# Chunk-selected attention with a gated causal convolution: the convolution cut into tiles of 64 by 32, output stores moved to ScalarE's queue, values loaded and cast by GpSimd's transfers

## The chip, the cores and the metric

The kernel runs on one core of a Trainium2 chip. The metric is the device time of one launch in microseconds (us). Before the change three runs took 195.68, 196.44 and 196.68 us, so the median is 196.44 us. The profile below is of a separate execution, whose span from the first to the last instruction is 196.0 us, with the TensorE clock fully granted throughout.

## What is computed

There are 4 sequences of 768 positions, 8 heads of 64 channels each. Every block of 32 keys is a chunk. Each query takes its six best chunks, by an upper bound of the score, and attends only to those (and only backwards in time). The heads laid side by side give `x` (4, 768, 512), and this goes through a gated unit: a causal convolution over five positions, channel by channel, gives the gate; `x @ w_val` gives the value; their product goes through `w_out`.

```python
k_min, k_max = min and max of k over each chunk of 32
ub = sum(maximum(q * k_min, q * k_max), axis=-1)         # bound of each chunk, per query
top_chunks = argsort(where(causal, ub, -1e9))[..., -6:]  # six chunks
scores = q @ k.T / sqrt(64), masked to those chunks and to the past
x = softmax(scores) @ v                                  # heads side by side: (4, 768, 512)

gate_pre = sum over k in 0..4 of conv_w[k] * xp[:, k:k + S, :]   # xp: x with four zeros ahead
gate = 1 / (1 + exp(-gate_pre))
out = (gate * (x @ w_val)) @ w_out
```

## The kernel before

Two heads are one pair; there are 16 pairs, four to a sequence. Each pair passes through the same stages. An operation is put on a list with its engine and its buffers, a list scheduler in the program orders all of them ahead of time, and each engine then runs its own fixed order. The keys of that order (`OFF`, `DELTA`, `PERIOD`) are tuned numbers. What runs when is fixed in the program; waits are only for data and buffers.

The loads and the cast of v:

```python
for x, name in enumerate(("kn", "qn", "vn")):
    G.op(f"{name}{p}", "SP", ..., load(name), w=[(name, p)], ...)       # SyncE's queue (L519, L522)

def vcast(p=p):                                                          # L639
    t.nc.gpsimd.tensor_copy(out=vv("VA", p)[:, :, :, 0:D], in_=vv("vn", p))
```

The selection mask is written twice, for two strips of rows (L716):

```python
for r in range(2):
    t.nc.vector.tensor_tensor(out=NS...[:, :, :, CH * r:CH * r + NCH], in0=src, in1=<sixth best>, op=ALU.is_lt)
```

Scores. The 2688 columns of a pair lie in six PSUM banks for each of its two heads (`BANKS`), and two banks make a `DUO`. Per duo, first all products of q and k in tiles of 64 rows (L748), two heads side by side in the array; then the mask is added as a product of 32 rows (L757), four tiles of 32 rows side by side:

```python
DUO = ((0, 1), (2, 3), (4, 5))
WIDTH = [512, 512, 512, 512, 384, 256]
...
for r, bi in enumerate(bs):
    ...
        for hh in range(2):
            t.nc.tensor.matmul(out=bank(("s", p, bi, hh))[:, col:col + n], lhsT=kh[HP[hh], ...], rhs=qh[HP[hh], q0:q0 + n], ...)
...
            for hh in range(2):
                rows = slice(64 * hh + 32 * r, 64 * hh + 32 * r + 32)
                t.nc.tensor.matmul(out=..., lhsT=t.E[rows, ...], rhs=mt[rows, ...], tile_position=(64 * hh + 32 * r, 0))
```

Then ScalarE takes the exponential (L766), GpSimd cuts the diagonal blocks (L774), TensorE multiplies by v (L797), VectorE normalizes (L806), and a transposing transfer puts the result into `xT` (L827).

The convolution is done on TensorE with diagonal weights, in one of two ways:

```python
CONV = "QQQQQQQQQQQSSSSQ"       # which of the ways each pair takes

# Q (L883): tiles of 64 rows by 64 columns, four side by side; needs the two halves of xT swapped (L849)
for k in range(2 * KSZ):
    for x, d in ((xT, 0), (XQ, 1)):
        for r in range(2):
            matmul(out=bank(("cv", p, r))[HP[r ^ d], 0:HB], lhsT=WQ[HP[r], ...], rhs=x[HP[r], a:a + HB])   # 40 of 384 columns

# S (L863): tiles of 128 rows by 32 columns, four side by side; needs four shifted copies, through DRAM
xw: scr[p % 4].rearrange("c (g n) -> g c n", g=4) <- xT        # L839, one transfer
xs: XS[blk::4] <- scr[p % 4]                                   # L845, four transfers
for w in range(2):
    for o in range(3):
        for g in range(4):
            matmul(out=bank(("cv", p, w))[32 * g:32 * g + 32, 0:HB], lhsT=WD[:, ...], rhs=XS[:, ...])       # 24 of 384 columns
```

Value and output, once for each sequence of four pairs: 8 groups of four matmuls with `w_val` (L913), the gate on VectorE (L921), 6 groups of four matmuls with `w_out` (L937), ScalarE takes them out of PSUM (L947; three of the 24 are VectorE's, L944), and SyncE's queue stores them:

```python
t.nc.sync.dma_start(out=t.out[b_, s * 128:(s + 1) * 128, :], in_=vv("osb", 6 * b_ + s))   # L952
```

In the first 26 us gaps of TensorE are filled with matmuls of zeros (L352, L1011).

Of the kernel before, what the change touches and what calls it, by code (L numbers as in the profile page):

```python
# [11 lines left out]
FP = mybir.dt.float32  # L12
# [7 lines left out]
CH = 32  # L20
# [4 lines left out]
KSZ = 5  # L25
NPAIR = B * H // 2
# [7 lines left out]
XN = S + 6  # L34

# [15 lines left out]

DUO = ((0, 1), (2, 3), (4, 5))
SCORE = [0.68, 0.70, 0.54]
# [3 lines left out]
for _bi, _segs in enumerate(BANKS):  # L57
    for _col, _jt, _q0, _n in _segs:
        for _i in range(_n // 128):
            WHERE[_jt, _q0 // 128 + _i] = (_bi, _col + 128 * _i)  # L60

NBUF = dict(kn=5, qn=5, vn=5, Kh=3, Qh=3, ql=2, rh=2, rl=2, km=2, KB=2, VA=3, mub=2, top=2, NS=2,
            MT=2, on=2, xT=8, XS=3, XQ=3, g=8, gv=8, osb=4, scr=4)

PERIOD = 12.9223
OFF = dict(wdg=199.168, wbig=-116.538, cw=-683.48, load=-91.162, ktr=-51.291, qtr=99.521, kev=-172.346,
           qev=175.061, ksm=-204.505, spl=464.719, vc=678.633, ub=-186.285, top=322.7, selT=-163.727,
           sc=-181.883, ex=-292.07, av=82.464, nrm=333.712, tox=-546.25, xs=-141.243, conv=13.848,
           tanh=-338.872, val=266.063, gv=171.155, out=288.504, ev=-184.148)
# [11 lines left out]
CONV = "QQQQQQQQQQQSSSSQ"  # L81

DELTA = dict(
    wdg=(-1.243, -0.346, -5.29, 3.059, -8.51, 0.295, -11.031, 1.615, 2.466, -0.239, -5.796, 0, -2.239, 11.59,
        -0.038, 0),
    wbig=(0, 0.188, -10.953, -0.19, 0.733, -1.414, -3.353, 1.285, -5.523, -4.485, 38.175, 5.823, 4.557,
        -13.478, 0.421, 0),
    cw=(-18.314, -8.891, -8.843, -0.026, -0.2, 7.762, 12.344, 5.613, 0.06, -2.242, -4.873, -3.047, -3.366,
        0.828, -9.749, -0.011),
    load=(0.214, -1.353, 0.394, -9.477, -20.991, -15.326, -0.566, -8.721, 0.066, -10.887, 23.08, 13.879, 6.207,  # L90
        -4.098, -7.797, -2.716),
    ktr=(3.721, -2.57, -4.059, 0.646, -13.55, 0, 0.055, -1.62, -0.373, 0.436, -1.532, 6.05, 2.065, 1.379, 2.36,
        0.267),
    qtr=(-5.316, -3.862, 0.606, 2.517, 0.494, 0.207, -0.25, -17.411, 1.198, 7.239, -4.482, 0.617, -1.715,
        -0.705, 1.938, 2.43),
    kev=(0, -2.085, -0.198, 0.772, 0.854, 1.732, -0.381, -2.561, 0.048, 6.873, -0.748, -3.931, -1.54, -5.598,
        0, 0),
    qev=(-0.006, -7.153, 2.8, -8.078, -1.913, -4.426, -6.52, -0.93, -1.584, 0.557, 6.224, 0.433, 0, 0.167,
        0.325, 1.843),
    ksm=(-0.516, 1.719, 1.719, 0, -8.166, 5.024, -7.553, -5.823, 0, -13.821, -3.788, 0, 0, 0, 6.169, -3.771),  # L100
    spl=(0, 0, 0.913, -1.823, 3.174, 0.698, 2.737, 0, -0.344, -1.736, -3.55, 8.03, 12.699, 0.056, 12.489, 1.296),
    vc=(-5.408, 8.102, -1.641, -3.236, -11.492, -2.331, -9.437, 2.42, -16.561, 6.032, 0, -2.029, 9.507, 2.124,
        11.374, 1.314),
    ub=(0, 5.87, -1.717, -6.846, -10.954, -7.75, -4.319, 18.215, 2.367, -3.332, -1.487, -3.834, 2.838, -3.08,
        -3.376, 6.316),
    top=(0.011, -14.157, -0.748, -6.694, 0, 1.128, -0.085, 25.804, -19.326, 6.323, 7.216, 7.115, 6.031, 0,
        17.873, -1.714),
    selT=(0.159, 4.322, -11.032, -3.664, 2.206, 2.91, 4.105, -0.067, 0, 2.718, -8.959, -6.512, 0.16, 8.002,
        -0.12, -1.732),
    sc=(2.402, 2.062, 3.966, 0.001, -31.282, -1.168, -3.404, 9.113, -1.06, 0.639, 4.728, -3.231, -1.122,  # L110
        -0.658, -0.515, 0.885),
    ex=(-2.337, 0.461, 5.963, 6.189, 0.222, 2.13, 5.144, 9.503, 6.939, 0.624, 0.959, -13.542, -6.471, -4.563,
        6.731, -4.322),
# [206 lines left out]
def graph(off, period, nbuf):  # L320
# [649 lines left out]
    for o in later:  # L970
        o.deps.add(byname["ksm1"])
# [170 lines left out]
```

## Time and profile before

| what | value |
|---|---|
| median of three runs | 196.44 us |
| span of the profiled execution | 196.0 us |
| TensorE (PE) busy | 184.8 us, 94% |
| VectorE (DVE) busy | 148.3 us, 76% |
| ScalarE (ACT) busy | 146.7 us, 75% |
| GpSimd (POOL) busy | 90.4 us, 46% |
| transfers | 36.01 MB, 94917 packets, of which 88226 are under 512 B |
| share of the 16 DMA engines' span taken by SyncE's queue | 74.5% |

A busy time says how long an engine had something in work, not that each piece was as fast as it could be; several matmuls overlap. What bounds the kernel is read from stretches of time: where one engine has no gap at all, its work sets the pace. The chain of work that ended last, and the waits of each engine, show the rest.

### The profile page before, as it was taken

The page shows a single profiled execution, that of the slowest core. Times are in us where ns is not written, and L with a number is a line of the kernel's source. Part 1 is how long each engine was busy: PE and PEld are TensorE (multiplying, and loading weights), DVE is VectorE, ACT ScalarE, POOL GpSimd, SP SyncE. Part 2 cuts the span into 40 slices and gives each one's busy share as a digit, 9 for nine tenths or more (in the row PEclk, how much of TensorE's full clock was granted, in tenths as well). Part 3 has the DMA queues.
Part 4 walks back from the last instruction along what each step waited for, and adds up shares of the span by engine and source line. Part 5 has one row for each costly group of instructions (what it writes and reads, how often), then busy time and mean ns, then how long its engine had stood idle before and what let it go on. Part 6 is the DMA issues. An engine that isn't in the chain of part 4 may idle for free.

```text
span 196.0 us, 7461 instructions
## 1 busy us (share of the span) xinstructions
PE 184.8 (94%) x2926; PEld 118.4 (60%) x2926; DVE 148.3 (76%) x476; ACT 146.7 (75%) x326; POOL 90.4 (46%) x189
## 2 busy tenths in 40 slices
PE   7989898979999999999999999999999997899992
PEld 3666666656757675686675677577656462555540
DVE  6897588979999988879998558998899614062451
ACT  4458999989778879895969897677988977633421
POOL 5589999888445344547262137414363212100000
PEclk9999999999999999999999999999999999999999
DMA  5999999989989998969796998230218839777225
GB/s 134 269 269 207 163 211 205 255 161 225 236 147 222 151 279 190 262 142 222 198 257 181 251 221 162 58 70 2 47 48 251 117 92 282 221 261 251 106 110 211
DMA packets 94917, 36.01 MB, mean 184 GB/s; under 512 B 88226, under 2 KB 91298, under 8 KB 94882
## 3 DMA queue, kind: packets, MB, share of 16 engines
q1 hardware_dynamic: 93826, 34.48, 74.5%
q0 software_dynamic: 1056, 1.05, 3.8%
q8 instruction: 23, 0.38, 0.8%
q14 instruction: 12, 0.10, 0.2%
HBM read 24.16 MB, written 7.08 MB: 159 GB/s over the span
## 4 chain that ended last, share of the span: by engine, by line
PE 74%; DVE 12%; DMA 5%; ACT 4%; SPq 2%; issue 2%; DVEq 0%
PE b L883 10%; PE b L913 10%; PE b L937 9%; PE b L797 9%; PE b L748 8%; PE b L534 8%; PE b L757 5%; PE b L652 5%; DMA xT<-on 3%; DVE km L546 3%; ACT P L766 2%; DMA XS<-scr 2%; PE b L726 2%; PE b L1011 2%; PE b L352 2%; DVE NS L716 2%
## 5 line engine op out<-in xcount | busy, mean ns | idle before, releaser
L766 ACT ACTIVATE P<-b 128x512 f16<-128x512 f32 (+1 forms) x192 | 88.9, 570 | 9.8 <-PE b L757 4.7
L774 POOL TENSOR_SCALAR_AFFINE_SELECT P<-P 128x512 f16<-128x512 f16 (+1 forms) x64 | 33.8, 550 | 60.5 <-ACT P L766 60.4
L546 DVE TENSOR_REDUCE km<-b 128x12 f32<-128x384 f32 x64 | 31.9, 548 | 6.7 <-PE b L534 2.8
L748 PE MATMUL b<-Qh,Kh 64*128 64x128 f16 (+3 forms) x384 | 28.8, 258 | 0.9 <-ACT P L766 0.4
L797 PE MATMUL b<-VA,P 128*128 128x65 f16 x672 | 28.0, 194 | 0.5 <-ACT P L766 0.4
L797 PEld LDWEIGHTS <-P 128*128 128x128 f16 x672 | 24.8, 98 | 4.1 <-issue 1.8
L921 DVE SCALAR_TENSOR_TENSOR gv<-g,b 128x384 f16<-128x384 f32 x32 | 17.5, 550 | 10.2 <-PE b L913 9.1
L913 PE MATMUL b<-xT,wval 128*128 128x384 f16 x128 | 23.8, 326 | 0.0
L937 PE MATMUL b<-wout,gv 128*128 128x512 f16 x96 | 23.5, 379 | 0.0
L947 ACT ACTIVATE osb<-b 128x512 f32<-128x512 f32 x21 | 12.8, 623 | 13.8 <-PE b L937 11.7
L889 ACT ACTIVATE g<-b 128x384 f32<-128x384 f32 x32 | 14.4, 495 | 10.2 <-PE b L883 7.6
L883 PE MATMUL b<-xT,WQ 64*64 64x384 f16 x240 | 21.8, 325 | 0.0
L883 PE MATMUL b<-XQ,WQ 64*64 64x384 f16 x240 | 21.8, 325 | 0.0
L540 ACT ACTIVATE Kh<-b 128x384 f16<-128x384 f32 x32 | 16.2, 520 | 7.0 <-PE b L534 5.2
L748 PEld LDWEIGHTS <-Kh 64*128 64x128 f16 x384 | 12.0, 94 | 12.8 <-issue 11.3
L806 DVE TENSOR_TENSOR on<-b,rcp 128x384 f16<-128x384 f32 x32 | 17.8, 557 | 1.1
L576 ACT ACTIVATE Qh<-b 128x384 f16<-128x384 f32 x32 | 15.7, 531 | 2.7 <-PE b L534 2.7
L757 PE MATMUL b<-MT,E 32*128 32x128 f16 (+4 forms) x352 | 17.6, 259 | 0.0
L883 PEld LDWEIGHTS <-WQ 64*64 64x64 f16 x480 | 12.8, 106 | 6.8 <-issue 2.0
L913 PEld LDWEIGHTS <-wval 128*128 128x128 f16 x128 | 11.5, 98 | 7.9 <-issue 1.3
L622 DVE SCALAR_TENSOR_TENSOR rl<-Qh,ql 128x640 f16<-128x640 f16 x16 | 15.9, 994 | 0.2
L534 PE MATMUL b<-ident,kn 128*128 128x128 f32 x96 | 15.1, 282 | 0.1
(102 smaller groups left out, 320.8 us busy)
## 6 DMA issues: line engine op xcount, KB each, us to landing
kn<-in_k_dram SPq DMA_DIRECT2D x32, 192.0 KB, 3.7
qn<-in_q_dram SPq DMA_DIRECT2D x32, 192.0 KB, 3.7
vn<-in_v_dram SPq DMA_DIRECT2D x16, 384.0 KB, 5.1
out_dram<-osb SPq DMA_DIRECT2D x24, 256.0 KB, 3.1
XS<-scr SPq DMA_DIRECT2D x16, 193.3 KB, 3.3
XQ<-xT SPq DMA_DIRECT2D x24, 96.8 KB, 2.5
scr<-xT SPq DMA_DIRECT2D x4, 193.5 KB
wval<-in_moe_w_val_dram POOLq DMA_DIRECT2D x1, 512.0 KB, 8.6
```

What stands on the lines that cost most here:

```text
L534: t.nc.tensor.matmul(out=b[:, j * 128:(j + 1) * 128], lhsT=vv(name, p)[:, 3 * w + j, :], rhs=t.ident, is_transpose=True, start=(j == 0), s ...
L546: t.nc.vector.tensor_reduce(out=vv("km", p)[:, i, w * 12:(w + 1) * 12], in_=bank(("kn", p, w))[:, 0:HB].rearrange("p (c t) -> p c t", t=CH ...
L748: t.nc.tensor.matmul(out=bank(("s", p, bi, hh))[:, col:col + n], lhsT=kh[HP[hh], jt * 128:(jt + 1) * 128], rhs=qh[HP[hh], q0:q0 + n], star ...
L757: t.nc.tensor.matmul(out=bank(("s", p, bi, hh))[:, col + m0 - q0:col + n], lhsT=t.E[rows, jt * 128:(jt + 1) * 128], rhs=mt[rows, m0 - 128: ...
L766: t.nc.scalar.activation(out=t.P[p % 2][hh][bi], in_=bank(("s", p, bi, hh))[:, 0:n], func=AF.Exp, scale=0.125 / QS)
L774: t.nc.gpsimd.affine_select(out=ap, in_=ap, pattern=[[0, n], [1, 128]], compare_op=ALU.is_ge, fill=0.0, base=0, channel_multiplier=-1)
L797: t.nc.tensor.matmul(out=b[:, qt, :], lhsT=t.P[p % 2][hh][bi][:, col:col + 128], rhs=vv("VA", p)[:, hh, jt, :], start=(jt == 0), stop=(jt ...
L806: t.nc.vector.tensor_tensor(out=vv("on", p)[:, :, hh * 64:(hh + 1) * 64], in0=b[:, :, 0:D], in1=rc.unsqueeze(2).to_broadcast([128, NT, D]) ...
L883: t.nc.tensor.matmul(out=bank(("cv", p, r))[HP[c], 0:HB], lhsT=t.WQ[HP[r], k // KSZ, k % KSZ, (p % 4) * 2 + c, :], rhs=x[HP[r], a:a + HB], ...
L913: t.nc.tensor.matmul(out=k[:, 0:HB], lhsT=t.wval[:, ct, et * 128:(et + 1) * 128], rhs=t.xT[:, (4 * b_ + ct) % 8, XL + w * HB:XL + (w + 1) ...
L921: t.nc.vector.scalar_tensor_tensor(out=vv("gv", 4 * b_ + et)[:, sl], in0=vv("g", 4 * b_ + et)[:, sl], scalar=1.0, in1=bank(("val", b_, et, ...
L937: t.nc.tensor.matmul(out=k, lhsT=vv("gv", 4 * b_ + et)[:, s * 128:(s + 1) * 128], rhs=t.wout[:, et, :], start=(et == 0), stop=(et == NCT - 1))
```

## The change

What it does and is for:

- **Convolution.** A new way R takes 15 of the 16 pairs (the last stays Q). It uses tiles of 64 rows by 32 columns, eight side by side. It needs two copies of `x`, in two halves of the sequence, which go through DRAM: one write with the 128 partitions as its outer dimension, instead of one with an outer dimension of 4, and four reads. The aim is less time on TensorE for each convolution.
- **Scores.** The duos go. Each of the six banks of a pair is a unit of its own, and the mask is added in tiles of 64 rows, as the products of q and k are. So the mask is written once on VectorE instead of twice.
- **Values.** The load of v and its cast to 16 bits become one transfer issued by GpSimd, which casts on the way. GpSimd's cast and the buffers of the uncast v go; `VA` has five buffers instead of three, k and q six instead of five.
- **Output stores** are issued by ScalarE, except for three of the last sequence.
- **Setup.** GpSimd builds the R weights in five pieces of 512 elements, and only the last pair's Q weights (two of 640 instead of ten of 512); the big weights and these come later.
- All keys of the schedule are tuned anew.

```diff
-NBUF = dict(kn=5, qn=5, vn=5, Kh=3, ..., VA=3, ...)
+NBUF = dict(kn=6, qn=6, Kh=3, ..., VA=5, ...)
-CONV = "QQQQQQQQQQQSSSSQ"
+CONV = "RRRRRRRRRRRRRRRQ"
 ... (PERIOD, OFF and DELTA: new numbers)
-        for x, name in enumerate(("kn", "qn", "vn")):
+        for x, name in enumerate(("kn", "qn")):
+        def vload(p=p, b_=b_, h0=h0):
+            for hh in range(2):
+                t.nc.gpsimd.dma_start(out=vv("VA", p)[:, hh, :, 0:D], in_=t.v[b_, h0 + hh].rearrange("(t p) d -> p t d", p=128))
-        def vcast(p=p):
-            t.nc.gpsimd.tensor_copy(out=vv("VA", p)[:, :, :, 0:D], in_=vv("vn", p))
 ... (mask)
-            for r in range(2):
-                t.nc.vector.tensor_tensor(out=...[:, :, :, CH * r:CH * r + NCH], ...)
+            t.nc.vector.tensor_tensor(out=...[:, :, :, 0:NCH], ...)
 ... (scores: one unit for each bank instead of each duo)
-                                rows = slice(64 * hh + 32 * r, 64 * hh + 32 * r + 32)
-                                t.nc.tensor.matmul(..., lhsT=t.E[rows, ...], rhs=mt[rows, ...], tile_position=(64 * hh + 32 * r, 0))
+                            nc.tensor.matmul(..., lhsT=t.E[HP[hh], ...], rhs=mt[HP[hh], ...])
 ... (convolution)
-            t.nc.sync.dma_start(out=t.scr[p % 4].rearrange("c (g n) -> g c n", g=4), in_=t.xT[:, p % 8, XL - 4:XL + S + 2])
+            t.nc.sync.dma_start(out=t.scr[p % 4], in_=t.xT[:, p % 8, XL - 4:XL + S])
+        def xs(r, p=p):
+                for blk in range(2):
+                    t.nc.sync.dma_start(out=vv("XS", p)[HP[r]][blk::2].rearrange("c (g n) -> c g n", g=4),
+                                        in_=t.scr[p % 4].rearrange("(g c) n -> c g n", g=4)[:, :, HB * r:HB * r + XH])
+        def conv(p=p):
+            for k in range(KSZ):
+                for g in range(4):
+                    for r in range(2):
+                        t.nc.tensor.matmul(out=bank(("cv", p, r))[32 * g:32 * g + 32, 0:HB],
+                                           lhsT=t.WD[HP[r], k * 16 + (p % 4) * 4 + g, :],
+                                           rhs=x[HP[r], g * XH + k:g * XH + k + HB], ...)
 ... (output)
-                t.nc.sync.dma_start(out=t.out[b_, ...], in_=vv("osb", 6 * b_ + s))
+                e = t.nc.sync if b_ == B - 1 and s % 2 else t.nc.scalar
+                e.dma_start(out=t.out[b_, ...], in_=vv("osb", 6 * b_ + s))
```

## The prediction

> **What bounds the kernel now.** I read the page's busy times first, then the stretches, then TensorE's own waits, then the chain.
>
> ```profile
> PE 184.8 (94%) x2926; PEld 118.4 (60%) x2926; DVE 148.3 (76%) x476; ACT 146.7 (75%) x326; POOL 90.4 (46%) x189
> ...
> DMA  5999999989989998969796998230218839777225
> ```
>
> The first line alone does not prove a TensorE bound: fillers and overlapping matmuls count as busy. The stretches do it. Columns: busy us of PE, its weight loads, DVE, ACT and POOL, then the granted clock, the DMA share and GB/s.
>
> ```profile
> 20.00:30.00 10.00, 9.10 (x180) 6.49 (x180) 7.75 (x37) 9.82 (x25) 9.51 (x17) 1.00 1.07 193
> 30.00:40.00 10.00, 9.13 (x175) 6.33 (x173) 9.31 (x28) 9.70 (x23) 9.37 (x15) 1.00 1.09 215
> ...
> 60.00:80.00 20.00, 20.00 (x358) 13.54 (x356) 18.20 (x61) 16.58 (x38) 9.46 (x22) 1.00 1.01 214
> 80.00:100.00 20.00, 20.00 (x346) 13.82 (x341) 18.45 (x59) 17.53 (x40) 9.33 (x20) 1.00 0.85 204
> ...
> 160.00:170.00 10.00, 7.96 (x129) 4.39 (x129) 2.34 (x6) 6.89 (x16) 1.31 (x3) 1.00 0.85 238
> ```
>
> There are three parts. Up to about 50 us no single engine is full: ACT, POOL and DVE take turns at 93 to 98%, and transfers are saturated. From 60 to 160 us TensorE has no gap, with DVE near 90%. After that TensorE is again the engine of the chain, with one hole, which the waits name (us in total, times, longest):
>
> ```profile
> PE b L863 <- DMA XS<-scr: 2.0, 1, 2.0
> PE b L352 <- DVE warm L346: 1.3, 1, 1.3
> PE b L726 <- DVE NS L716: 0.7, 2, 0.4
> ```
>
> So after 50 us a microsecond taken from TensorE is nearly a microsecond of the kernel, as long as the others keep up. The chain in order of time gives the price of its pieces (start, us, what):
>
> ```profile
> 67.80 0.38 PE b L748 x8
> 68.45 0.42 PE b L797 x10
> ...
> 90.79 0.55 PE b L748 x12
> 91.64 1.83 PE b L937 x8
> 93.47 0.54 PE b L748 x4
> 94.33 0.79 PE b L652 x20
> ...
> 103.67 1.75 PE b L883 x40
> ...
> 171.83 1.10 PE b L863 x24
> ```
>
> One Q convolution is 1.75 us, one S convolution 1.10 to 1.17. From the start of a duo to the next piece gives the scores with their mask: 91.64 - 90.79 = 0.85, 94.33 - 93.47 = 0.86, 68.45 - 67.80 = 0.65, in all 2.36 us a pair.
>
> **What the Trainium skill says.** (1) "TensorEngine Tiling (Array Packing)", Available Configurations, lists 64x32 as eight tiles; its Key Properties say that a change of tiling mode drains the engine. The trace agrees: forty Q matmuls of 384 columns, four side by side, need 10 x 384 / 2.4 = 1600 ns of columns (2.4 GHz is the clock that the next page gives) and take 1.75, so about 0.15 us goes at the ends. (2) "TensorE: Matmul & The Clock Gate", section Wait — 56ns, not 53.3ns?, gives about 25 ns as the least distance between matmul starts. Here sixteen small ones (L667) take 0.39 us in the chain, 24 ns each: it agrees. (3) "DMA: Bandwidth & Descriptors", Issuing engines are not separate DMA queues: another issuer saves only issue time, the 16 engines are shared. No run here has stores on ACT yet.
>
> **The change part by part.**
>
> *Convolution.* Eight tiles: 5 x 384 / 2.4 = 0.80 us, plus 0.15 at the ends, 0.95. But 40 matmuls in 0.80 us are 20 ns apart, below the 24 ns just seen: 40 x 24 = 0.96, plus 0.15, 1.11. I take the middle, 1.05 (estimate). Eleven Q become R: 11 x (1.75 - 1.05) = 7.7. Four S become R: 4 x (1.15 - 1.05) = 0.4. **8.1 us off TensorE**, all of it after 50 us.
>
> *Scores.* Now: 2688 product columns at two heads side by side are 1.12 us; the masks over queries from 192 on are 2432 columns a head, in four tiles about 0.56 us (the longer bank of each duo: 448, 512 and 384). Sum 1.68 against 2.36 measured: 0.68 over three duos is lost, which I put down to drains when the tiles go from 64 to 32 rows and back. After: 2688 + 2432 = 5120 columns are 2.13 us, without a change inside a bank. The built program has 49 runs of score matmuls on TensorE against 45 before, so some three entries a pair at about 0.11 each: 2.13 + 0.34 = 2.47. **16 x 0.11 = 1.8 us on.** The choice to drop the duos then costs little, because half of what they saved went in drains.
>
> *DVE.* The mask is written once: half of 24 x 457 + 8 x 399 ns, **7 us off DVE**. From 60 us this is hidden, but it keeps DVE below TensorE at the faster pace: (148.3 - 7) / 16 is 8.8 us a pair, and TensorE's own, without 9.5 us of fillers (3.6 + 5.9) and the 6.3 us net found here, is (184.8 - 15.8) / 16 = 10.6. Before 50 us it counts.
>
> *Start.* k and q of the second pair no longer stand behind a v (0.63 us of issue, 384 KB) in SyncE's queue. GpSimd, 95% full from 20 to 40 us, loses ten Q weight pieces (10.9 us) and the casts (0.83 each), and gains five of about 1.1 and issues. DVE is on the path from 30 to 50 us and saves 0.4 a pair there. **About 2 us off** (estimate, my softest term).
>
> *Values.* The cast goes: 16 x 0.83 = 13.2 us off POOL. 32 issues of 768 rows come; the two weight loads took POOL 0.94 and 0.75 us each, so some 29 us on. POOL ends near 100 of 190 us: free enough. Same packets read, half the bytes written.
>
> *Detour.* Per pair R moves 198 KB out and 4 x 99 KB back, Q swapped 194 KB: 11 x 0.4 - 4 x 0.37 (S moved 967 KB) = +2.9 MB, less 3.1 MB of v written. Near neutral in bytes.
>
> *Stores.* SyncE needs 0.42 to 0.5 us for one. If ACT's queue stands still as long, 21 x 0.45 = 9.5 us, about half of it after 160 us, where ACT is idle. ACT is at 82 to 88% before, so most hides; I add 1.
>
> Sum: -8.1 + 1.8 - 2 + 1 = -7.3, and I take 0.3 back for waits that the new fixed order meets: 196.4 - 7.0 = **189.4 us**.
>
> **Rivals.**
>
> *A: the detour becomes the wait.* Fifteen convolutions now need transpose, write, read in a row, and the DMA share is already about 1.0 from 60 to 80 us. Every landing adds: 2.9 (transpose), about 3 (write: the page has no landing for it, I take it like the read) and 3.3 us (read), and the one wait of TensorE on a transfer now is of this kind (2.0 us). For it: the order is fixed, and a late read stops TensorE at once. Against it: SyncE is relieved of v and stores, the write spreads over 128 outer rows instead of 4, and transfers fall to 11% busy around 135 us, so there is room in total. If it happens a few times: 193 to 197.
>
> *B: ACT becomes the bound.* At a 4% faster pace 85% becomes 89, with 0.45 us a store and its wait for the copy out of PSUM some 94%. Exponentials free the PSUM banks that TensorE needs. Time 191 to 194.
>
> *C: matmuls of 64x32 overlap fully and the start gains more.* R at 0.95 gives 9.6 off instead of 8.1; a start 4 us shorter gives 184 to 186.
>
> *D: casting transfers are slow.* If a packet that casts takes twice the 25 ns mean of now (74.5% of 16 x 196 us over 93826 packets), 24576 of them add 38 us to each engine's 156, and loads come late: above 196. No trace here has small casting packets.
>
> **Range and chances.** The TensorE terms are firm to about 2.5 us; the start is between 0 and 4 off, A and B together between 0 and 5 on. That gives 183.5 to 194.5. Faster by over 2% means below 192.5: 0.78. Within 2%: 0.15. Slower takes A or D in full: 0.07.
>
> **What would show it.** R convolutions at 1.0 to 1.1 us each in the chain; scores near 2.5 us a pair; TensorE without gaps from about 50 us on, fewer us busy in all (near 176: 6.3 of work and some fillers less); DVE near 141; ACT's waits ahead of exponentials short. Wrong it would be by TensorE waits on XS above 4 us in total, by R above 1.3 us, by waits for VA, or by ACT full while TensorE has gaps.

## The result and the profile after

The changed kernel takes **202.24 us** (median of 4 runs, 201.75 to 202.76) where the kernel before took 196.56 beside it: a ratio of 1.030, with an interval of 1.025 to 1.035. It is 5.7 us slower; 189.4 was predicted, and the range ended at 194.5.

First the same two lines of the profile's page that the prediction showed of before, busy times and the slices of the DMA engines, then the page's queues (packets, MB, and their packets' time as a share of 16 engines' span), all of the changed kernel:

```profile
PE 181.0 (90%) x2982; PEld 120.1 (60%) x2982; DVE 138.6 (69%) x456; ACT 144.7 (72%) x326; POOL 97.6 (49%) x200
...
DMA  6999999999999999999979999998941675544325
...
q1 hardware_dynamic: 73714, 25.47, 70.3%
q0 software_dynamic: 26144, 4.20, 30.6%
q10 hardware_dynamic: 3024, 5.51, 7.6%
```

The DMA engines were near full until about 120 us and rested around 135; now they are near full until 145. q1 is SyncE's, q0 GpSimd's and q10 ScalarE's. Together the queues' packets took 109% of the engines' span (79% before, nearly all SyncE's), although the bytes hardly changed: 35.65 MB after 36.01. Over 100% means that packets of different queues were under way at once on one engine.

TensorE's stretches of the changed kernel (columns as in the prediction):

```profile
60.00:80.00 20.00, 19.33 (x393) 14.24 (x390) 18.79 (x72) 17.70 (x42) 16.39 (x33) 1.00 1.58 185
80.00:100.00 20.00, 19.20 (x409) 14.04 (x407) 15.60 (x53) 16.08 (x38) 9.66 (x19) 1.00 1.48 191
100.00:120.00 20.00, 15.30 (x247) 9.44 (x246) 10.28 (x33) 11.80 (x26) 7.80 (x18) 0.94 1.04 207
120.00:140.00 20.00, 20.00 (x317) 13.06 (x316) 14.66 (x42) 14.04 (x32) 5.71 (x12) 0.98 1.17 214
```

Where TensorE had no gap it now has 4.7 us of them between 100 and 120 us, the two longest 2.4 and 1.7 us; DVE, ACT and POOL fall too: everybody waits. Below, the two together are called the hole. The chain of the changed kernel, in order of time, names what ended the longer one, and one convolution later on (start, us, what):

```profile
110.34 0.57 SPq L510
110.92 0.05 issue
110.97 4.91 DMA kn<-in_k_dram
115.87 0.02 issue
115.89 0.02 ACTq L936
...
116.34 0.50 ACT g L872
116.83 0.04 issue
116.88 0.47 PE b L779 x10
...
131.87 0.94 PE b L846 x40
```

A load of k goes out late, at 111 us, and lands at 115.9. What waits for it is no transpose but ACTq L936, a store in ScalarE's stream. Behind the store stand the gate's tanh (L872), and behind that TensorE, 2.44 us. Why a store waits for a load of k is told by the waits of the built program, two transfers of SyncE's and the store:

```
L510 DMACopy kn0_133<-in_k_dram 128x6x64       [waits DMAHW2_49]
L510 DMACopy kn0_133<-in_k_dram 128x6x64       [waits DMAHW3_49]
L936 DMACopy out_0_dram<-osb2_200 128x512      [waits DMAHW3_49,Activation_49]
```

In the built program the 182 transfers of SyncE and ScalarE report their landing on eight counters, DMAHW0 to 7, in turn. Before a transfer may use a counter, its issuer waits until the transfer that used it last has landed, whatever that was; the store is the eighth transfer after the second of these loads. So at most eight of these transfers can be under way, and how fast they land sets how fast the next go out. Stores on ScalarE bring that wait into the engine that makes exponentials.

The timeline of SyncE's queue shows why k went out late (start, us, what; a group of transfers with its own waits):

```profile
93.72 1.17 SPq L510 DMA_DIRECT2D kn<-in_k_dram  x2
94.93 2.37 SPq L510 DMA_DIRECT2D qn<-in_q_dram  x2
97.34 2.06 SPq L510 DMA_DIRECT2D kn<-in_k_dram  x2
99.50 7.31 SPq L826 DMA_DIRECT2D XS<-scr  x8
106.85 0.59 SPq L821 DMA_DIRECT2D scr<-xT  x1
107.55 2.74 SPq L809 DMA_TRANSPOSE xT<-on  x2
110.34 1.18 SPq L510 DMA_DIRECT2D kn<-in_k_dram  x2
```

From 93 to 111 us SyncE has no free moment. Eight reads of the detour, a write and two transposes, 10.6 us of queue, stand between two loads of k. And the transfers are slower: k's median from issue to landing went from 3.7 to 4.7 us, q's from 3.7 to 5.8, the transposes' from 2.9 to 4.4. The runs will show that for k and q this second part comes mostly with the loads of v, and not with the detour.

### The profile page after: what moved, and what is told of

It reads as the page before. It is cut to its first block, busy times and chain, and to the rows that moved or that the text cites. A ratio compares the mean times of both kernels' runs of the same rounds, so it can differ in the third digit from the quotient of the medians.

```text
span 200.1 us, 7601 instructions
## 1 busy us (share of the span) xinstructions
PE 181.0 (90%) x2982; PEld 120.1 (60%) x2982; DVE 138.6 (69%) x456; ACT 144.7 (72%) x326; POOL 97.6 (49%) x200
## 2 busy tenths in 40 slices
DMA packets 102917, 35.65 MB, mean 178 GB/s; under 512 B 89058, under 2 KB 99810, under 8 KB 102882
## 3 DMA queue, kind: packets, MB, share of 16 engines
q1 hardware_dynamic: 73714, 25.47, 70.3%
## 4 chain that ended last, share of the span: by engine, by line
PE 53%; DMA 16%; ACT 9%; SPq 9%; DVE 7%; issue 3%; ACTq 0%; DVEq 0%
PE b L920 10%; PE b L896 9%; PE b L736 7%; DMA qn<-in_q_dram 7%; PE b L527 6%; ACT P L750 6%; PE b L779 6%; PE b L741 5%; PE b L846 5%; SPq L510 5%; DMA XS<-scr 4%; SPq L826 3%; DMA scr<-xT 3%; DMA kn<-in_k_dram 2%; PE b L641 2%
## 5 line engine op out<-in xcount | busy, mean ns | idle before, releaser
L750 ACT ACTIVATE P<-b 128x512 f16<-128x512 f32 (+2 forms) x192 | 89.7, 632 | 7.5 <-PE b L741 6.8
L736 PE MATMUL b<-Qh,Kh 64*128 64x128 f16 (+3 forms) x384 | 39.9, 258 | 1.0 <-issue 0.8
L741 PE MATMUL b<-MT,E 64*128 64x128 f16 (+4 forms) x352 | 37.2, 255 | 1.3 <-DVE MT L722 1.3
L779 PE MATMUL b<-VA,P 128*128 128x65 f16 x672 | 27.9, 194 | 3.2 <-ACT g L872 2.4
L518 POOL DMA_DIRECT2D VA<-in_v_dram x32 | 27.2, 855 | 6.7 <-PE b L779 6.4
L779 PEld LDWEIGHTS <-P 128*128 128x128 f16 x672 | 24.9, 98 | 8.8 <-issue 7.1
L736 PEld LDWEIGHTS <-Kh 64*128 64x128 f16 x384 | 18.2, 94 | 12.3 <-issue 8.1
L872 ACT ACTIVATE g<-b 128x384 f32<-128x384 f32 x32 | 14.6, 524 | 14.9 <-PE b L846 7.7
L896 PE MATMUL b<-xT,wval 128*128 128x384 f16 x128 | 25.3, 334 | 0.0
L930 ACT ACTIVATE osb<-b 128x512 f32<-128x512 f32 x21 | 12.7, 618 | 13.7 <-PE b L920 10.6
L741 PEld LDWEIGHTS <-E 64*128 64x128 f16 x352 | 17.6, 94 | 6.2 <-issue 3.6
L846 PE MATMUL b<-XS,WD 64*32 64x384 f16 x600 | 16.0, 324 | 3.7 <-DMA XS<-scr 2.0
L527 PE MATMUL b<-ident,qn 128*128 128x128 f32 x96 | 14.6, 281 | 2.2 <-DMA qn<-in_q_dram 2.2
L527 PE MATMUL b<-ident,kn 128*128 128x128 f32 x96 | 14.1, 279 | 1.2 <-DMA kn<-in_k_dram 1.2
```

The lines of the kernel that those rows point to most:

```text
L518: t.nc.gpsimd.dma_start(out=vv("VA", p)[:, hh, :, 0:D], in_=t.v[b_, h0 + hh].rearrange("(t p) d -> p t d", p=128))
L527: t.nc.tensor.matmul(out=b[:, j * 128:(j + 1) * 128], lhsT=vv(name, p)[:, 3 * w + j, :], rhs=t.ident, is_transpose=True, start=(j == 0), s ...
L736: nc.tensor.matmul(out=bb[hh][:, col:col + n], lhsT=kh[HP[hh], jt * 128:(jt + 1) * 128], rhs=qh[HP[hh], q0:q0 + n], start=(si == 0), stop= ...
L741: nc.tensor.matmul(out=bb[hh][:, col + m0 - q0:col + n], lhsT=t.E[HP[hh], jt * 128:(jt + 1) * 128], rhs=mt[HP[hh], m0 - 128:q0 + n - 128], ...
L750: t.nc.scalar.activation(out=t.P[p % 2][hh][bi], in_=bank(("s", p, bi, hh))[:, 0:n], func=AF.Exp, scale=0.125 / QS)
L779: t.nc.tensor.matmul(out=b[:, qt, :], lhsT=t.P[p % 2][hh][bi][:, col:col + 128], rhs=vv("VA", p)[:, hh, jt, :], start=(jt == 0), stop=(jt ...
```

## The experiments

Two theories at first. **Transfers**: the detour and the loads of v fill the queue and the engines that k and q need. **TensorE**: the new matmuls or their order cost what the prediction had counted as saved. The last is soon out: the chain's convolution of 0.94 us is better than predicted. So the runs ask which transfers, and by what: SyncE's time to issue, or the packets. Each run gives the median of all its executions and a ratio to the kernel before, run on the same chip; the changed kernel is 1.030. Some executions show a lower TensorE clock or a longer time than the rest, and the ratios leave these out; where too few remain, no ratio is given. Differences in us are worked out from the ratios, times 196.6 us. (Expectations that quote earlier runs took differences of medians: 7.9 us for v, 10.8 to 12.3 for the detour, 4 for the stores.)

### Loads of v left out

The changed kernel; from the sixth pair on v isn't loaded, and later pairs multiply old values.

```diff
         def vload(...):
+            if p >= nbuf['VA']:
+                return
```

> The changed kernel with the loads of v left out from the sixth pair on (old values stay in the buffers); every engine's order as in the changed kernel. Theory V (GpSimd's casting transfers crowd the 16 engines and make k and q land late): the hole of TensorE from 100 to 120 us closes, k and q land in about 3.7 us as in the kernel before, 192 us or less. Theory D (the detour's transfers are the excess): 197 to 200. Theory L (k and q stand too late in SyncE's order): 197 or more, since their place is the same.

Measured: 194.33 us, ratio 0.983 (0.979 to 0.986). 9 us come back, and the landings of k and q fall to 4.1 and 4.4 us.

### The detour left out

The changed kernel; from the fourth pair on, scratch writes and reads aren't made, and convolutions use old copies.

```diff
         def xw(p=p):
+            if p >= nbuf['XS']:
+                return
         def xs(r, p=p):
             def emit():
+                if p >= nbuf['XS']:
+                    return
```

> The changed kernel with the detour's writes and reads left out from the fourth pair on (convolutions take old data); all orders kept. Theory D: k and q land in about 3.7 us, the hole closes, 192 us or less. Theory V: 197 to 200. Theory L: also faster, since SyncE has some 35 us less to issue ahead of the loads, but k and q still land slowly: 194 to 197.

Measured: 191.44 us, ratio 0.973 (0.965 to 0.981): 11 us come back, and TensorE has no gap from 100 to 180 us. The two parts together would give 20 us if they were separate costs.

One half of the expectation failed. The loads of k and q land no sooner than in the changed kernel (4.7 and 5.8 us there; the last number is the median from issue to landing):

```profile
kn<-in_k_dram SPq DMA_DIRECT2D x32, 192.0 KB, 5.1
qn<-in_q_dram SPq DMA_DIRECT2D x32, 192.0 KB, 5.7
```

So the hole closes although the landings stay slow; leaving v out had brought them down. What changes here is when the loads are issued, the last of them at 132.5 us and not at 139.3 as in the changed kernel.

### v by SyncE again

The changed kernel, with v loaded by SyncE and cast by GpSimd as before; the order on TensorE, ScalarE and VectorE is kept. Pair 13 multiplies an older v, because its cast comes after its use.

```diff
-        def vload(...): nc.gpsimd.dma_start(out=VA, in_=v)
+        nc.sync.dma_start(out=vn, in_=v)
+        def vcast(...): nc.gpsimd.tensor_copy(out=VA, in_=vn)
```

> The changed kernel with v loaded uncast by SyncE and cast by GpSimd, as before the change; the orders of TensorE, ScalarE and VectorE kept. Theory V: 193 to 196. Theory D: 199 to 203, as the same packets are still moved. Theory L: 203 or more, since SyncE gets 16 more transfers ahead of its loads.

Measured: 208.5 us, ratio 1.057 (1.047 to 1.068), 5 us slower than the changed kernel. Beside this detour, GpSimd's transfers are the lesser evil. It has one waste in it (16 more issues in a full queue), so it says nothing of v alone.

### Loads of k and q earlier

The changed kernel; the loads of pairs 8 to 15 stand up to 20 us earlier in SyncE's order.

```diff
-    return G, t, G.schedule(), full
+    return G, t, earlier(G.schedule()), full      # LEAD = 20.0
```

> The changed kernel with the loads of k and q of pairs 8 to 15 put up to 20 us earlier in SyncE's order, nothing else moved. Theory L: the hole of 100 to 120 us closes, 193 to 196. Theories V and D: the transfers are full anyway, so the detour comes late instead: 200 to 204.

Measured: 211.1 us (206.75 to 213.77), with no ratio; the fastest execution is still 4 us above the slowest of the changed kernel. The theory that the loads only stand too late in the order finds no support: put forward, they hold up the detour instead. TensorE's waits in an execution of 212 us:

```profile
PE b L846 <- DMA XS<-scr: 7.2, 5, 2.5
PE b L641 <- DVE on L788: 4.5, 1, 4.5
```

In the changed kernel's own order the wait for XS was 2.0 us. What one transfer gains another loses.

### A thin detour

The changed kernel; all the detour's transfers are issued and waited for, but from the fifth pair (writes) and the fourth (reads) with 1/16 of the rows, so that convolutions use partly old copies.

```diff
-  ... dma_start(out=t.scr[p % 4], in_=t.xT[:, ...])
+  n = 8 if p >= nbuf['scr'] else 128
+  ... dma_start(out=t.scr[p % 4][0:n], in_=t.xT[0:n, ...])     # reads: 2 rows of 32
```

> The changed kernel with every write and read of the detour still issued and waited for, but from the fifth pair (writes) and the fourth pair (reads) on with a sixteenth of the rows, so that almost no data moves. If what the detour costs is the data on the 16 engines: 191 to 193, as with the detour left out. If it is SyncE's time to issue 75 transfers and the extra links of its chain: 198 to 202, as with the whole change.

Measured: 194.59 us, ratio 0.985 (0.978 to 0.992). Of the 11 us some 9 go with the data; the other 2, with issues and waits, are within the spread of the two runs. Its SyncE timeline for the same stretch:

```profile
97.96 5.27 SPq L828 DMA_DIRECT2D XS<-scr  x8
...
106.43 1.23 SPq L510 DMA_DIRECT2D kn<-in_k_dram  x2
```

The eight reads hold the queue 5.3 us instead of 7.3, and the next k goes out 3.9 us sooner: with fewer packets to move the queue moves faster. Whether transfers also land sooner can't be read from this trace.

### Stores by SyncE again

```diff
-                e = t.nc.sync if b_ == B - 1 and s % 2 else t.nc.scalar
+                e = t.nc.sync
```

> The changed kernel with all output stores issued by SyncE at the places where ScalarE issued them. If the stores held ScalarE up: 199 or less. If SyncE's queue is the narrow place, as the run with v put back into it suggests: 204 or more. If neither: 201 to 203.

Measured: 198.39 us, ratio 1.004 (1.001 to 1.007). So in the changed kernel stores by ScalarE cost about 5 us, more than the 1 predicted. That is about the size of the hole, which came through two such stores: 2.4 us behind the one shown, and 1.7 behind one that stood until an XS had landed.

### The kernel before, with v by GpSimd alone

The kernel before; v by GpSimd's casting transfers where SyncE loaded it, six buffers, no cast.

```diff
-        nc.sync.dma_start(out=vn, in_=v);  nc.gpsimd.tensor_copy(out=VA, in_=vn)
+        nc.gpsimd.dma_start(out=VA[p % 6], in_=v)
```

> The kernel before with one part of the change alone: v loaded and cast by GpSimd's transfers at the places where SyncE loaded it, six buffers for it, no cast; all other orders kept. If casting transfers crowd the engines: 199 or more. If they relieve SyncE's queue, as the run with v put back suggests: 193 to 196. Else within 1 us of 196.6.

Measured: 202.47 us, ratio 1.029 (1.024 to 1.033): by itself this part costs as much as the whole change. TensorE's first wait, and the stretch of 20 to 40 us, of this run:

```profile
PE b L797 <- POOL P L774: 5.3, 5, 2.4
...
20.00:40.00 20.00, 15.21 (x316) 11.43 (x313) 13.20 (x55) 16.78 (x40) 19.23 (x29) 0.99 1.17 164
```

GpSimd issues 32 transfers at 0.85 us each; here its stretch is full, its cuts of the diagonal (L774) come late, and TensorE waits for them. In the same 20 us TensorE was busy 18.23 us before. The landings of k and q, 3.7 us each before, are 4.4 and 4.8 us in this run, with no new detour in it: slower landings come with these loads of v. In the changed kernel, where GpSimd builds fewer weights, no wait of TensorE names GpSimd.

### The kernel before, with half of Q's work left out

The kernel before; the 12 Q convolutions leave out the correcting half of their weights, 20 matmuls instead of 40.

```diff
-            for k in range(2 * KSZ):
+            for k in range(KSZ):
```

> The kernel before with the second, correcting half of the twelve Q convolutions left out (weights of 16 bits only), so that each takes about 0.95 us instead of 1.75; no transfer and no order changed. If a microsecond of TensorE is a microsecond of the kernel as long as transfers don't grow (the first claim of the prediction): 12 x 0.8 = 9.6 us less, 187 to 189. If VectorE, ScalarE or the loads take over as the bound: 191 to 195.

Measured: 194.03 us, ratio 0.984 (0.979 to 0.990). TensorE has about 12 x 0.8 = 9.6 us less to do, and the kernel gains 3. One stretch suggests the next limit, VectorE at 18.68 of 20 us (18.45 before); it is from the slowest execution of this run, 196.15 us:

```profile
80.00:100.00 20.00, 19.81 (x313) 13.58 (x310) 18.68 (x60) 17.13 (x39) 10.11 (x22) 1.00 1.06 234
```

### The same, with the second mask copy left out

```diff
-            for r in range(2):        # mask, L716
+            for r in range(1):
```

> The kernel before with the correcting half of the 12 Q convolutions left out (9.6 us less TensorE work, which alone brought only about 3 us), and with the second copy of the block mask left out on VectorE, as the changed kernel has it (0.3 to 0.45 us per pair, some 6 us of VectorE in all). The second mask rows then keep old contents; the work on TensorE is the same. Theory VectorE (with TensorE relieved, VectorE at 18.7 to 18.9 of 20 us is what holds the kernel before): 188 to 191 us, 3 to 6 us below the run without the mask change. Theory transfers (with TensorE relieved, loads and the swap's landings hold it): 193 to 195 us, within 1 us of that run.

Measured: 191.43 us, ratio 0.975 (0.967 to 0.983). The mask, which the prediction had called hidden after 60 us, seems to bring some 2 us more once TensorE is relieved; the two intervals overlap, so this is likely and not shown. Together the two are worth 5 us.

### The kernel before, with stores by ScalarE

```diff
-                t.nc.sync.dma_start(out=t.out[b_, ...], in_=osb)
+                e = t.nc.sync if b_ == B - 1 and s % 2 else t.nc.scalar
+                e.dma_start(out=t.out[b_, ...], in_=osb)
```

> The kernel before with one part of the change: output stores issued by ScalarE at the places where SyncE issued them, every second of the last batch's by SyncE. Theory ScalarE: ScalarE is busy about 70 to 75 percent, and each store puts a wait for the output copy and 0.34 us of issue into its stream, so 1.5 to 4.5 us slower, 198 to 201 us. Rival (a hidden cost because TensorE has slack against ScalarE in the kernel before): within 1 us, 196 to 197.5 us.

Measured: 198.38 us, ratio 1.006 (1.003 to 1.008): 1.1 us by the ratio. Both theories had missed it a little; the prediction's 1 us holds in the old order.

### The changed kernel without detour

The changed kernel in its own order; each convolution is done as Q with the upper half of the weights alone, 20 matmuls, with the swap where the detour's reads stood. It leaves out the correcting half, so weights count as 16-bit numbers, as x does.

```diff
         def conv(p=p):
+            return convq(p)
 ... convq
-            for k in range(2 * KSZ):
+            for k in range(KSZ):
 ... detour: xw gone; xs(r):
+                t.nc.sync.dma_start(out=vv("XQ", p)[HP[1 - r], :], in_=t.xT[HP[r], p % 8, XL - 4:XL + S + 2])
```

> The changed kernel in its own order, with the detour gone for all pairs: every convolution is done in 64-by-64 tiles as the old Q form, but with the upper 16-bit half of the weights alone, 20 matmuls of 384 columns where Q had 40 and the new form has 40 half-sized ones. So TensorE's work per convolution is about half of Q's 1.75 us, 0.9 us, the same as the new form's 0.94, and the only traffic is the swap of two halves inside SBUF (0.39 MB written per pair in place of 0.19 + 0.39 MB written and as much read). Theory transfers (the detour's packets crowd out the loads of k and q): as in the run that left the detour out from the fourth pair on, 190 to 192.5 us, landings of k and q between the old 3.7 and the new 4.7 to 5.8 us, and TensorE without the hole at 100 to 120 us. Theory GpSimd (casting loads of v are what holds the kernel): within 3 us of the changed kernel, 199 or more. Theory TensorE-mode (the tiles of 64 by 32 themselves slow the stream of matmuls): 188 to 190 us, with 100 to 180 us less than the earlier run by the drains.

Measured: **189.92 us**, ratio 0.962 (0.953 to 0.971). With the two runs that follow it is the fastest of the study. Its stretch of 100 to 120 us, and one convolution in its chain:

```profile
100.00:120.00 20.00, 19.87 (x251) 12.32 (x249) 14.42 (x44) 15.71 (x37) 11.12 (x25) 1.00 1.10 172
...
80.72 0.94 PE b L857 x20
```

A convolution takes 0.94 us here as in the changed kernel, and v, stores, scores and mask are the changed kernel's. So the new order and its savings are good for 7 us, once the detour is gone. Most of that is the shorter convolution and the single mask: the kernel before with both (191.43 us, ratio 0.975) is some 2.6 us behind, and the two intervals overlap. As with the detour left out, k and q land no sooner, 5.0 and 5.7 us after issue.

### The same, with stores by SyncE

```diff
-                e = t.nc.sync if b_ == B - 1 and s % 2 else t.nc.scalar
+                e = t.nc.sync
```

> The same without the detour, and with all the output stores issued by SyncE at the same places instead of ScalarE. Theory ScalarE (a store in ScalarE's stream costs its 0.34 us of issue and its wait, about 20 times, in the path of exponentials and evictions): 3 to 4 us under the run beside it, about 187 to 188.5 us, as the stores alone were worth 4 us in the changed kernel. Rival (the stores only mattered because everything behind them was already late through the detour): within 1 us of the run beside it, 190 to 192 us. Rival (SyncE's issues delay the loads once it has stores again): 0 to 2 us slower.

Measured: 190.33 us, ratio 0.967 (0.961 to 0.972), no gain. The 5 us that stores cost beside the detour are gone. ScalarE's waits name no transfer, with stores (the run before this one) or without: when it comes to a store, the counter is free.

### Without detour and without v

The kernel without detour, with v left out from the sixth pair on as in the first run.

```diff
         def vload(...):
+            if p >= nbuf['VA']:
+                return
```

> The kernel without the detour (convolutions in 64-by-64 tiles with the upper half of the weights, 189.9 us) with the loads of v left out as well from the sixth pair on, so that later pairs multiply by older values. In the changed kernel leaving v out was worth 7.9 us and leaving the detour out 10.8 to 12.3 us; what is to be told apart is whether these are two costs or one. Theory sharing (both act through the same full DMA engines, and one relieved leaves room for the other): v is now worth at most 2 us, 188 to 190 us. Theory GpSimd (the casting loads cost by GpSimd's own issue time and packets, whatever else is in flight): 5 to 8 us more, 182 to 185 us.

Measured: 189.23 us, ratio 0.963 (0.959 to 0.967): nothing is gained. With the detour, v was worth 9 us; without it, none, although k and q now land 4.5 and 4.7 us after issue. So the two aren't separate costs. Whether they meet in the DMA engines isn't shown by this: without the detour TensorE has no gap worth naming from 80 us on, and then a load that lands sooner has nothing to give.

### The kernel before, with a detour's traffic added

The kernel before; where it issues a swap, four reads of the size and pieces of the new detour are added in nine pairs, and four scratch writes. Nobody waits for the data.

```diff
         def swap(p=p):
             ...
+            if p < 11:
+                if p < 4:
+                    nc.sync.dma_start(out=dscr[p % 4], in_=xT)
+                if p >= 2:
+                    (four times) nc.sync.dma_start(out=XS[p % 3] half, in_=dscr[(p - 2) % 4])
```

> The kernel before in its own order, with the detour's traffic added and nothing else: in 9 of its first 11 pairs, where the swap is issued, four more transfers of 97 KB from DRAM scratch to the buffers of the shifted copies, in the pieces that the changed kernel reads, and four writes of the scratch for a start; nobody waits for the data, and TensorE's work is unchanged. About 4.3 MB more, all before the loads of k and q end. Theory transfers (packets of the detour crowd the loads out, whoever uses them): 3 to 7 us slower, 200 to 204 us, landings of k and q above 4.2 us (3.7 before). Theory chain (the detour costs by its two landings in a row ahead of the convolution, not by its bytes): within 1 us, 196 to 198 us.

Measured: 213.56 us, ratio 1.088 (1.083 to 1.093). Far more than expected, and not in the expected way: k and q land in 3.7 and 3.8 us, as before. What changed is when they are issued. v in SyncE's queue, in the kernel before and then in this run (ns of one issue, least/median/most; first and last start):

```profile
L519 SPq DMA_DIRECT2D vn<-in_v_dram x16: 386/628/1373, 3.5 to 116.8; - x16
```

```profile
L519 SPq DMA_DIRECT2D vn<-in_v_dram x16: 380/638/5033, 3.5 to 133.9; - x16
L856 SPq DMA_DIRECT2D XS<-dscr x36: 588/612/1627, 57.7 to 148.3; - x36
```

40 added transfers at 0.61 us are 24 us of SyncE's time. The last v goes out 17.1 us later, and the kernel is 17 us longer. The order has no place made for these transfers; one tuned with them might pay less.

### The same, thin

As before, with 2 rows of 32 in each added read.

```diff
-   ... XS[...][blk::2] <- dscr[...][:, :, ...]
+   ... XS[...][blk:4:2] <- dscr[...][0:2, :, ...]
```

> The run of the kernel before with the extra detour traffic (213.6 us), with the 36 added reads cut from 32 rows to 2 each: the same number of transfers is issued by SyncE at the same places, with 1/16 of the data; the four writes of the scratch stay. In that run k and q landed as fast as in the kernel before (3.7 and 3.8 us), but SyncE issued 40 transfers more at about 0.61 us each, 24 us in all, and the last v was issued at 133.9 us instead of 116.8. Theory issue (the time in SyncE's queue is what costs): still 208 to 214 us. Theory data (the packets cost, through full DMA engines): 197 to 202 us.

Measured: 210.22 us, ratio 1.067 (1.055 to 1.079). 13 of the 17 us stay without the data. TensorE's first wait of this run:

```profile
PE b L891 <- DMA XQ<-xT: 8.2, 5, 2.4
```

In the old order the cost of a detour is mostly SyncE's time, and it comes out as waits for swaps that are issued late. The kernel before had no such wait among its longest.

### The loads of k by ScalarE

The changed kernel; the last ten pairs' k is issued by ScalarE at the same places.

```diff
-                    t.nc.sync.dma_start(out=dst[...], in_=src[hh]...)
+                e = t.nc.scalar if name == "kn" and p >= 6 else t.nc.sync
+                    e.dma_start(out=dst[...], in_=src[hh]...)
```

> The changed kernel with the loads of k of the last ten pairs (20 transfers, 0.62 us of issue each in SyncE's queue) issued by ScalarE at the same places of the order; same packets, same buffers, same computation. Theory issue (SyncE's queue in order, full from 50 to 130 us, is what makes the changed kernel late): 12 us leave SyncE's queue and some 7 to 12 us of issue enter ScalarE, which was 72 percent busy; the last q is issued 5 us or more before 139 us and the kernel takes 194 to 199 us. Theory packets (the full DMA engines set when data lands, whoever issues): the loads land no sooner, ScalarE's added issues cost, 201 to 207 us.

Measured: 213.19 us, ratio 1.084 (1.076 to 1.092). Worse than either theory had it, and by another mechanism. The chain of this run (start, us, what):

```profile
97.80 5.74 DMA XS<-scr
103.56 0.38 ACTq L511
104.03 0.50 ACTq L511
```

A landing of the detour holds up a load of k in ScalarE's stream, for the same reason as the stores: the counter isn't free. ScalarE's exponentials stand behind it. k lands later as well, 5.5 us after its issue in the median instead of 4.7.

### Half of the detour's reads by ScalarE

```diff
-                    t.nc.sync.dma_start(out=vv("XS", p)...
+                    e = t.nc.scalar if blk else t.nc.sync
+                    e.dma_start(out=vv("XS", p)...
```

> The changed kernel with every second read of the detour (30 of 60, 0.60 us of issue each) issued by ScalarE instead of SyncE at the same places; same packets and computation. These reads wait for the landing of the scratch's write, in ScalarE's stream now. Theory issue: 18 us leave SyncE's queue, so k and q are issued earlier, 195 to 200 us, unless ScalarE's waits for the writes stop the exponentials. Theory packets: 201 to 206 us.

Measured: 201.16 us (196.83 to 203.71). The times lie too far apart for a verdict: the median is about that of the changed kernel, and one execution is 5 us below it. A gain from this is neither shown nor excluded.

### The detour in fewer transfers

The changed kernel at full precision; two writes lay the scratch out so that one read of 388 KB fills all the copies. It makes three transfers a pair instead of five, with the same data in the copies.

```diff
-   nc.sync.dma_start(out=scr, in_=xT)                              # 1 write
+   for r in range(2): nc.sync.dma_start(out=scr[r].rearrange("c g n -> g c n"), in_=xT[..., half r])
-   (four times) nc.sync.dma_start(out=XS[HP[r]][blk::2], in_=scr rows of 388)
+   nc.sync.dma_start(out=XS, in_=scr.rearrange("r c g n -> (r c) (g n)"), each row twice)
```

> The changed kernel with its own convolution at full precision, order and issuers, and the detour packed anew: two writes of 99 KB lay the scratch out by half, channel and group, and one read of 397 KB, each scratch row of 3104 B going to two rows of the shifted copies, takes the place of four reads of 97 KB in rows of 776 B. Three transfers a pair in place of five, the same bytes into the copies, fewer and larger packets. Each of SyncE's and ScalarE's transfers waits for one of eight counters, so for the landing of a transfer about eight places earlier; fewer transfers turn these over less often. Theory transfers (issue time, packets and the eight counters, all in the stretch of 40 to 130 us): 192 to 197 us, with q1's share below 65 percent and the hole of 100 to 120 us under 2 us. Theory chain (the detour costs by write and read in a row ahead of the convolution): 200 to 204 us, as now.

Measured: 206.58 us (204.48 to 208.64) where the kernel before took 197.13. A miss: no faster than the changed kernel's 202.24. q1's packets still take 71.1% of the engines' span (70.3 in the changed kernel), since the bytes are the same and only 4680 of q1's 73714 packets went. With the thin detour this suggests that in the changed kernel the data count more than the number of transfers. It doesn't show it, because the large read brings a cost of its own: it stands in SyncE's queue until its write has landed, twice for 5.0 us in all.

## Why the prediction was wrong, step by step

**"After 50 us a microsecond taken from TensorE is nearly a microsecond of the kernel": wrong.** The prediction guarded itself with "as long as the others keep up". They don't: 9.6 us less on TensorE gave 3 us, and 5 with the mask. Lines with 20.00 of 20.00 show that TensorE always had something in work, and not that the others had reserve. VectorE at 18 of 20 stood in the same lines; "near 90%" is too much for the whole of 60 to 160 us, though, since from 100 to 120 us it was 14.2 of 20 and from 140 to 160 us 15.0.

**Convolution: better than predicted.** 0.94 us against 1.05, which is rival C's 0.95. The prediction had put the Trainium skill's least distance of about 25 ns between matmul starts ("TensorE: Matmul & The Clock Gate", section Wait — 56ns, not 53.3ns?) beside the columns. The small matmuls of L667, which use the whole array, keep it in the trace, 25 ns apart. Tiles that lie side by side don't: the first eight of a convolution start within 40 ns, 3 to 4 ns apart, and the next eight some 150 ns later. And 20 matmuls in tiles of 64 by 64, in the run without detour, take the same 0.94 us as these 40. So the columns and the ends set the time here, not the distance. Eleven times 0.81 and four times 0.2 give 9.7 us off.

**Scores: wrong, and harmless.** By the mean time of a score matmul in the chain, 57 to 60 ns in both kernels, times the 46 of a pair, they took about 2.7 us before and take as much now. The 2.36 of the prediction had come from three picked pieces, and no run shows the drains that it read from them. Whether its 0.11 was added is too fine for this reckoning.

**VectorE: right in size** (9.7 us less busy, 7 predicted); "hidden" is in doubt, by the run without the second mask copy.

**Start: not seen.** By 40 us both kernels had done 84 of the 672 products with v (L797 before, L779 now); of the 384 score products (L748, L736) the kernel before had done 84, the changed one 72.

**Values: right in GpSimd's time, wrong in what the transfers do.** GpSimd ends at 97.6 us busy, as predicted, and its 32 issues take 27.2 us (29 predicted). "Free enough" failed in the old order, where they lie in stretches in which GpSimd was full, with 5.3 us of TensorE's waits; in the changed kernel no wait of TensorE names GpSimd. What v does there is to slow the landings of k and q, which fall from 4.7 and 5.8 us to 4.1 and 4.4 without it. That is rival D's direction, and not its size. q0's packets without those of the weights and of the first five pairs' v, from the first run, took 36.6 ns each (17248 packets in 980 - 349 us), against 24.9 for q1 before: not double. But q1's own packets now take 30.5 ns, and 28.0 when v is left out.

**Detour: "near neutral in bytes" is the step that failed.** It priced the detour at nothing; the runs show 11 to 13 us in the changed kernel. The sum of bytes holds, 35.65 MB against 36.01, and SyncE's transfers didn't grow in number either, 165 before and 161 now, since v and 21 stores left it. Both are beside the point, because they count over the whole run. S made its detour from 140 us on, when the loads were done (last v at 116.8 us); R makes it from 38 to 181 us, in the stretch where the engines were full already. Up to the last load of k or q SyncE now issues 129 transfers, which hold its queue for 118.7 us, where it issued 114 with 99.9 us, and that last load goes out at 139.3 us instead of 116.1. The old order shows what places in this queue can cost by themselves, 13 us for 40 issues with 1/16 of the reads' data; the changed kernel's order pays mostly for the data, some 9 of 11 us.

Rival A had the mechanism and its argument ("the DMA share is already about 1.0 from 60 to 80 us"), and then set against it the room around 135 us, which no transfer of 60 to 120 us can use. Its size (4 to 8 us over the forecast) was too small. And its sign was looked for in the wrong place: TensorE's wait for XS was 2.0 us and not "above 4". The delay came out in loads that are issued late, and in stores that wait for a landing.

**Stores: right in the old order (1.1 us), 5 us beside the detour, none without it.** The prediction priced the issue alone, 0.45 us each (it is 0.34). The wait for a counter was not in it: ScalarE stood 2.8 us for one store until a load of k had landed. The Trainium skill's "DMA: Bandwidth & Descriptors", section Issuing engines are not separate DMA queues, says that more issuers save only the time to initiate, usually small relative to the DMA. The loads of k on ScalarE agree with its first half: they landed no sooner. The second half needs this case's numbers: 0.6 us of issue against 2.7 us to landing, as for the reads added to the kernel before, isn't small where 40 of them stand in one queue.

**The sum.** Without the detour, the rest of the change gives 189.9 us, which is the prediction's 189.4 in all but the detour. That is partly luck: TensorE's time and the mask were worth 5 us together in the old order, where the prediction had 8.1 and nothing, and the start brought none of its 2.

What stays open: by what the detour's data cost, whether in the engines or by holding SyncE's queue, because thin packets also let the queue move faster. Whether more than eight counters would help was not tried, nor how the order would come out if it were tuned without the detour.

## What to carry to other kernels

Ask of a new transfer in which stretch it runs, how many issues it adds to which queue, and what has to land before it may be issued; the sum of bytes over the run answers none of these. A full engine is not a bound that pays back one for one: look in the same line for the second-fullest engine. A cost that vanishes when another part is left out, as those of v and the stores did here, isn't that part's own, so look for the part that makes it matter and keep the rest: the changed kernel with swaps and 16-bit weights beats both kernels, if 16 bits are enough for the weights.

## What the runs showed of the hardware that was not expected

- The eight tiles of 64 by 32 run side by side: eight matmuls of 384 columns start 3 to 4 ns apart, the next eight some 150 ns later, and forty of them take 0.94 us, as twenty in tiles of 64 by 64 do.
- Transfers of 97 to 193 KB in short rows hold SyncE's queue for about 0.6 us each, with 1/16 of the data too (0.59 in the thin detour), and a read of 388 KB as long (0.58); the output stores, 256 KB each, hold a queue 0.34 us, SyncE's or ScalarE's. The loads of k held ScalarE's queue only 0.40 us each in the run that moved them, the reads of the detour 0.59.
- A GpSimd transfer of 768 rows holds GpSimd 0.86 us, about what its cast of a whole pair took (0.83), and a pair needs two.
- Loads of v by GpSimd slow the landings of others: k and q went from 3.7 us each to 4.4 and 4.8 in the kernel before with only that part changed.
- One and the same transfer can hold the queue much longer: a read of scratch up to 2.0 us, where 0.57 is the least. The runs don't show why.
